# A linear-attention and soft-MoE kernel: a new start, a new task order, and the last expert's second layer split

## The chip, the core and the metric

The kernel runs on one core of a Trainium2 chip. The time is device microseconds of one execution; the figure for a kernel is the median of its runs. For the kernel before that is 119.74 us (three runs: 119.74, 120.53, 118.95).

## What is computed

An RWKV-like recurrence over 4 batches, 8 heads, 768 time steps and head size 48, and then a soft mixture of 8 experts with 4 slots each over the 3072 resulting rows of width 384:

```python
for t in range(S):
    cur = np.einsum('bhd,bhe->bhde', u[None] * kt, vt)
    y[:, :, t] = np.einsum('bhd,bhde->bhe', rt, state + cur)
    state = w[None, :, :, None] * state + np.einsum('bhd,bhe->bhde', kt, vt)
x = y as (3072, 384)
logits = x @ phi                                   # 3072 x 32
d = softmax(logits, over rows);  slot_input = d.T @ x
slot_out[e] = relu(slot_input[e] @ w1[e]) @ w2[e]  # w1 384 x 1024, w2 1024 x 384, 8 experts
c = softmax(logits, over slots)
out = c @ slot_out
```

All inputs are f32 in HBM, as is the output (3072 x 384, 4.7 MB). The inputs r, k, v are 14.2 MB and w1, w2 25.2 MB.

## The kernel before

The recurrence is done in chunks of 128 steps: twelve chunk steps `n` (`step`, L498), two batches at a time in the two halves of the partitions. Two chunks make a unit `U` (six units). Of each unit r, k and v are loaded by two loads each (36 loads of 128 x 768, `load`, L333), issued by POOL with a cast from f32 to bf16. `turned` (L438) transposes each 48-wide piece on TensorE (L447); VectorE multiplies the transposed k and r by tables of powers of w while it moves them out of PSUM (L458), ScalarE copies v (L455). Then, for each chunk: k and v are turned back per head (`normal`, L485), the scores k.r are made and masked (L512, L517), the current step's own term comes from u (L531, L563), y is summed in PSUM (L580 to L587) and copied to `x` (L594), the state is advanced (L543 to L557), `x` is transposed in three blocks of 128 columns (L609), copied (L612), and multiplied with phi into logits (L628). `tab`, the tables, hold the powers of w: w and u are loaded into `wu` (L344 to L347, twice each: for the two halves of the partitions), transposed by TensorE (L399), and their logarithm is multiplied by iota values and exponentiated (L407, L410). `ident_f`, the identity for transposes, is built by POOL (L352, L353).

`combine` makes the softmax over slots and its transpose `LexpT`; `dispatch` sums the slots' inputs over groups of chunks with a running maximum; `finish_slots` folds them into `uns` (L823, L828). `first_layer` (L863 to L889) makes `h` for two groups `g` of four experts and its transpose `hT`; its results stand in partitions 32j to 32j+31 for expert j of a group. `second_layer` (L905) multiplies `hT` by w2: for each of 8 y, four experts at a time, each in its own 32 columns of the array, all 384 wide, into one PSUM bank. ScalarE scales the sum by the slots' denominators into `so` (L910). `output` multiplies `LexpT` by `so` into 24 tiles of 128 x 384 (L934), which VectorE and ScalarE copy in turn (L936, L938) and SP stores in pieces of 1, 2, 3, 4, 4, 4, 4, 2 tiles (L940).

The weights are loaded by POOL as well, w1 first (L847) and then w2 (L850), 768 KB each in bf16, with a cast. w2 of expert e lies where loads 4e to 4e+3 of r, k, v lay. A load waits until the load 5 (or 7) places before it in the order of their creation has landed.

The order of all work is made by `Plan`: each piece is a `task` with a priority, an engine, a duration, what it reads, writes and uses. `order` runs a list schedule over these, with corrections per task in `TUNE`, and `emit` issues the tasks in the resulting order and puts fill matmuls (`idle`, L922) where TensorE would be free before the first chunk and after the last y.

Because every engine works through its own instructions in order, the order of emission is the order on each engine; POOL's loads stand in one row with its arithmetic (L471, L557).

Of the kernel before, what the change touches and what calls it, by code (L numbers as in the profile page):

```python
# [7 lines left out]
LAT = {"PE": 0.22, "DVE": 0.25, "ACT": 0.25, "POOL": 0.28, "SP": 0.1}  # L8
SAME = {"PE": 0.0, "DVE": 0.12, "ACT": 0.12, "POOL": 0.12, "SP": 0.0}


class Plan:
# [4 lines left out]
    def __init__(self, tune):  # L17

        self.tune = tune
        self.tasks, self.pools, self.writers, self.readers, self.users = [], {}, {}, {}, {}  # L20
        self.slot, self.landed = {}, []
# [30 lines left out]
    def order(self):  # L52
        tasks, free, end = self.tasks, {}, {}
# [8 lines left out]
        while ready:  # L62
            best = None
            for i in ready:
# [51 lines left out]
        return [i for _, _, i in sorted(out)]  # L116

    def emit(self, where, fill, took=0.22):
# [11 lines left out]
TUNE = {46: (0.6, 0.0), 47: (-0.81, 0.2), 48: (-0.47, 0.0), 49: (1.82, 0.0), 50: (-0.25, 0.2), 73: (-2.02, 0.0),   # L130
# [82 lines left out]
def kernel(  # L213
# [14 lines left out]
    C = 128  # L228
# [130 lines left out]
    for U in range(1, UU):  # L359
        for which in range(3):  # L360
            load(U, which)
# [28 lines left out]
    for b_ in banks:  # L390
        task(-150, "PE", 0.4, lambda b_=b_: clear(b_), r=["warm"], w=["cleared"], n=1)
# [600 lines left out]
```

## Time and profile before

| | us |
|---|---|
| median of 3 runs | 119.74 (118.95 to 120.53) |
| the profiled execution | 118.71 |
| its span | 116.9 |
| TensorE busy | 99.7 (85%) |
| VectorE busy | 92.9 (80%) |
| ScalarE busy | 78.4 (67%) |
| POOL busy | 72.6 (62%) |
| bytes moved by DMA (as written) | 24.70 MB |

The profiled execution's own time holds 1.8 us outside the span. Busy shares are means over stages: the recurrence up to about 84 us, a chain of small steps with the two layers up to about 101 us, and the output. A granted clock of 1.00 is TensorE's full speed. In the rows by stretch each engine's busy time comes with its instructions (x), then the granted clock, the share that the 16 DMA engines were busy (over 1 where transfers overlap), and GB/s written. A cast load reads twice the bytes that it writes.

### The profile page before, as it was taken

The page shows a single profiled execution, that of the slowest core. Times are in us where ns is not written, and L with a number is a line of the kernel's source. Part 1 is how long each engine was busy: PE and PEld are TensorE (multiplying, and loading weights), DVE is VectorE, ACT ScalarE, POOL GpSimd, SP SyncE. Part 2 cuts the span into 40 slices and gives each one's busy share as a digit, 9 for nine tenths or more (in the row PEclk, how much of TensorE's full clock was granted, in tenths as well). Part 3 has the DMA queues.
Part 4 walks back from the last instruction along what each step waited for, and adds up shares of the span by engine and source line. Part 5 has one row for each costly group of instructions (what it writes and reads, how often), then busy time and mean ns, then how long its engine had stood idle before and what let it go on. Part 6 is the DMA issues. An engine that isn't in the chain of part 4 may idle for free.

```text
span 116.9 us, 4280 instructions
## 1 busy us (share of the span) xinstructions
PE 99.7 (85%) x1844; PEld 71.7 (61%) x1844; DVE 92.9 (80%) x152; ACT 78.4 (67%) x159; POOL 72.6 (62%) x111
## 2 busy tenths in 40 slices
PE   5979999999998999999989998999899995655200
PEld 1354587778786788777868777787665552445100
DVE  6789599999999999999999899999975561086400
ACT  4261878788789697895888898889764750175400
POOL 6999848999999999894769945999111010000000
PEclk9999999999999999999999999999999999999955
DMA  2999999999999999999999999999999994059994
GB/s 10 171 187 198 208 206 205 209 205 209 206 207 209 230 209 212 223 210 221 214 208 224 210 220 210 214 219 216 208 219 216 210 219 98 0 196 410 419 421 170
DMA packets 9122, 24.70 MB, mean 211 GB/s; under 512 B 1424, under 2 KB 6160, under 8 KB 9104
## 3 DMA queue, kind: packets, MB, share of 16 engines
q0 software_dynamic: 7488, 19.66, 87.2%
q1 hardware_dynamic: 1584, 4.77, 10.4%
q8 instruction: 14, 0.23, 0.7%
q14 instruction: 4, 0.03, 0.1%
q10 hardware_dynamic: 32, 0.00, 0.0%
HBM read 39.38 MB, written 4.72 MB: 377 GB/s over the span
## 4 chain that ended last, share of the span: by engine, by line
PE 32%; POOL 27%; DMA 24%; issue 4%; DVE 4%; ACT 2%; DVEq 0%; POOLq 0%
DMA raw<-in_moe_w_dram 17%; POOL raw L339 12%; PE T L447 8%; POOL arena L471 7%; DMA raw<-in_k_dram 7%; POOL Z L557 5%; PE T L485 5%; PE Ab L512 3%; DVE arena L936 3%; PE Y L580 2%; PE T L609 2%; ACT arena L938 2%; PE Y L587 1%; PE Sb L531 1%; PE Y L585 1%
## 5 line engine op out<-in xcount | busy, mean ns | idle before, releaser
L458 DVE TENSOR_TENSOR arena<-T,tab 128x1024 bf16<-128x1024 bf16 x24 | 29.0, 1217 | 2.5 <-PE T L447 2.2
L517 DVE TENSOR_TENSOR arena<-Ab,mask 128x1024 bf16<-128x1024 f32 x24 | 29.2, 1216 | 0.9 <-PE Ab L512 0.8
L447 PE MATMUL T<-by_head,raw 128*48 128x128 bf16 x576 | 22.8, 221 | 1.2 <-DMA raw<-in_r_dram 0.7
L471 POOL TENSOR_TENSOR arena<-arena 128x1024 bf16<-128x1024 bf16 x10 | 21.4, 2136 | 0.6 <-DVE arena L458 0.5
L447 PEld LDWEIGHTS <-raw 128*48 128x48 bf16 x576 | 16.9, 102 | 6.4 <-issue 3.3
L557 POOL TENSOR_TENSOR Z<-Ss,wCm 128x384 bf16<-128x384 f32 x20 | 16.7, 841 | 5.1 <-ACT Ss L554 5.0
L455 ACT COPY arena<-T 128x1024 bf16<-128x1024 bf16 x12 | 12.2, 1017 | 3.7 <-PE T L447 3.5
L594 ACT CAST x_all<-Y 128x384 bf16<-128x384 f32 x23 | 11.1, 489 | 1.6 <-PE Y L587 1.5
L485 PE MATMUL T<-ident,arena 112*128 112x112 bf16 x176 | 12.0, 213 | 0.1
L554 ACT COPY Ss<-Y 128x384 f32<-128x384 f32 x20 | 9.7, 491 | 3.0 <-PE Y L547 2.7
L563 DVE TENSOR_TENSOR dv<-vn,Sb 128x768 bf16<-128x768 bf16 x12 | 11.3, 946 | 0.2
L489 ACT COPY vn<-T 128x768 bf16<-128x768 bf16 x12 | 9.7, 811 | 2.4 <-PE T L485 2.2
L612 ACT COPY xT<-T 128x768 bf16<-128x768 bf16 (+2 forms) x13 | 9.7, 758 | 1.3 <-PE T L609 1.0
L485 PEld LDWEIGHTS <-arena 112*128 112x128 bf16 x176 | 9.3, 97 | 1.5 <-DVE arena L458 0.3
L512 PE MATMUL Ab<-arena 48*128 48x128 bf16 x192 | 9.7, 219 | 0.3 <-issue 0.3
L664 POOL TENSOR_TENSOR Le<-E,rs 128x128 bf16<-128x128 f32 x6 | 2.4, 400 | 11.5 <-PE Ab L863 5.9
L580 PE MATMUL Y<-vn,arena 128*128 128x48 bf16 x192 | 8.8, 184 | 0.2 <-DVE arena L517 0.2
L489 ACT COPY kn<-T 128x768 bf16<-128x768 bf16 x10 | 8.0, 805 | 0.8 <-PE T L485 0.7
L339 POOL DMA_DIRECT2D raw<-in_k_dram x12 | 6.5, 554 | 2.4 <-DMA raw<-in_v_dram 1.4
L587 PE MATMUL Y<-dv,ident 128*128 128x384 bf16 x24 | 7.8, 325 | 0.0
L580 PEld LDWEIGHTS <-arena 128*128 128x128 bf16 x192 | 6.8, 96 | 1.4 <-DVE arena L517 0.3
L512 PEld LDWEIGHTS <-arena 48*128 48x128 bf16 x192 | 5.5, 94 | 3.1 <-issue 1.6
(146 smaller groups left out, 197.9 us busy)
## 6 DMA issues: line engine op xcount, KB each, us to landing
w_all<-in_moe_w_dram POOLq DMA_DIRECT2D x8, 768.0 KB, 17.7
raw<-in_moe_w_dram POOLq DMA_DIRECT2D x8, 768.0 KB, 20.6
out_dram<-arena SPq DMA_DIRECT2D x4, 768.0 KB, 5.6
raw<-in_k_dram POOLq DMA_DIRECT2D x12, 192.0 KB, 6.9
raw<-in_r_dram POOLq DMA_DIRECT2D x12, 192.0 KB, 7.0
raw<-in_v_dram POOLq DMA_DIRECT2D x12, 192.0 KB, 7.2
out_dram<-arena SPq DMA_DIRECT2D x2, 384.0 KB, 2.4
out_dram<-arena SPq DMA_DIRECT2D x1, 576.0 KB, 2.9
```

The costliest lines, as they stand in the source:

```text
L339: pool.dma_start(out=raw_of(which, U, x), in_=ap)), w=[("raw", 6 * U + 2 * which + x)], dma=0.97, lag=7)
L447: O(pe.transpose(T[64 * x:64 * x + D, C * j:C * j + C], raw_of(which, U, x)[:, jj * D:(jj + 1) * D], by_head[:]))
L455: O(act.copy(dst, src))
L458: O(dve.tensor_mul(dst.rearrange("p j (h c) q -> p j h c q", c=2), src.rearrange("p j (h c) q -> p j h c q", c=2), tb[:, :, :, None, :].to ...
L471: O((pool if U else dve).tensor_mul(pr_t[P["pr", 2 * U + b]].rearrange("p (h a) -> p h a", h=H), kt, rt))
L485: O(pe.transpose(T[:, h * C:h * C + 64 + D], cell(st[P[src, U]], h, cc)[0:64 + D], ident[0:64 + D, 0:64 + D]))
L489: O(act.copy(nt[P[name, n]][:].rearrange("p h x d -> p (h x) d")[:, :, 0:D], T[:].rearrange("p (a d) -> p a d", d=64)[:, :, 0:D]))
L512: O(pe.matmul(Ab[:, x, i * C:(i + 1) * C], cell(kt, 4 * rd + i, cc)[s], cell(rt, 4 * rd + i, cc)[s], start=True, stop=True))
L517: O(dve.tensor_mul(AT[:, :, 4 * rd:4 * rd + 4, :], Ab[:].rearrange("p x (h t) -> p x h t", h=4), mask[:, None, None, :].to_broadcast([128, ...
L557: task(n + 0.2 + 0.05 * hh, "POOL", 0.8, lambda hh=hh: O(pool.tensor_mul(Z_t[P["Z", (n, hh)]][:], Ss_t[P["Ss", (n, hh)]][:], wCm[:, 4 * hh ...
L563: O(eng.tensor_mul(dv_t[P["dv", n]][:].rearrange("p h x d -> p (h x) d"), vn_t[P["vn", n]][:].rearrange("p h x d -> p (h x) d"), sums[:, : ...
L580: O(pe.matmul(Y[:, (2 * i + x) * D:(2 * i + x + 1) * D], AT[:, x, h, :], vn[:, h, x, :], start=(i == 0 and x == 0), stop=False, skip_group ...
```

## The change

- **First v.** Load 4 of the 36 (v of the first unit, first batch) is issued by SP, without a cast, into f32 space in `AT_t[0]`, and cast by ScalarE into its place. It is SP's first instruction; phi follows. The other 35 are still POOL's.
- **w and u.** Each has its own tile, `w_in` and `u_in`, of 8 partitions, and comes by one load on ScalarE's queue that reads it twice; SP loads neither. They are transposed and copied each by itself, and the logarithm needs w alone.
- **ident_f** is built by POOL ahead of its first load, not behind the first two.
- **phi** is loaded with three consecutive rows per partition (128 pieces of 384 bytes in place of 384 of 128). So the transposes of x take every third column.
- **Order.** `TUNE` is empty; a list `SEQ` gives the order of all 613 tasks. On each engine it differs from before throughout. Among other things POOL's loads of r of the last unit stand ahead of r of the second unit; VectorE makes all four table products before its first product with data, and casts phi, clears x's ones, one `Le` and one `E` later, between the chunks; and only two clears of PSUM and a fill stand before w's transpose. The bank of `Sb` is cleared on a key of its own.
- **Last chunk's xT.** Its first third is copied by VectorE, and both parts of its transpose wait for both halves of x.
- **w2 of the last expert** is loaded in two parts, y 0 to 5 and y 6 to 7.
- **Second layer.** The fourth expert of each group is taken out of the row of four: its matmuls are made in two halves of 192 columns, into two other PSUM banks (`rest`), the other three as before (`most`). Behind the last part of w2 come two matmuls for each half. `so` is scaled in three pieces: 96 partitions by ScalarE, and the last 32 partitions half by ScalarE, half by VectorE.
- **Output.** The first tile is made and copied in two halves, by ScalarE and VectorE; the stores are of 1, 1, 1, 2, 3, 4, 4, 4, 4 tiles.

```diff
+            if i == 4:
+                st = AT_t[0].bitcast(f32)[:, 0:JD]
+                task(-220, "SP", 4.5, lambda ap=ap: O(sp.dma_start(out=st, in_=ap)), r=["sp"], w=["st", "sp"])
+                task(-95, "ACT", 0.83, lambda: O(act.copy(raw_of(2, 0, 0), st)), r=["st"], w=[("raw", 4)])
...
-    task(-200, "SP", 1.2, lambda: O(sp.dma_start(out=wu[0:8, 0, 0:D], in_=w)), r=["wu0"], w=["wuA"])
-    task(-200, "SP", 1.2, lambda: O(sp.dma_start(out=wu[8:16, 0, 0:D], in_=u)), r=["wu0"], w=["wuB"])
-    task(-200, "ACT", 1.2, lambda: O(act.dma_start(out=wu[0:8, 1, 0:D], in_=w)), r=["wu0"], w=["wuC"])
-    task(-200, "ACT", 1.2, lambda: O(act.dma_start(out=wu[8:16, 1, 0:D], in_=u)), r=["wu0"], w=["wuD"])
+    task(-210, "Q", 2.05, lambda: O(act.dma_start(out=w_in[:, :, 0:D], in_=both(w))), w=["wA"])
+    task(-210, "Q", 2.0, lambda: O(act.dma_start(out=u_in[:, :, 0:D], in_=both(u))), w=["uA"])
...
-                        O(pe.transpose(T[:, o:o + C], xx[:, x, mi * C:(mi + 1) * C], ident[:]))
+                        O(pe.transpose(T[:, o:o + C], xx[:, x, mi:Dm:nM], ident[:]))
...
+        def most(g, y0, y1):
+            for y in range(y0, y1):
+                for j in range(EL):
+                    O(pe.matmul(SO[32 * j:32 * j + 32, :], hT[g][:, y, 32 * j:32 * j + 32], w2_of(g * EG + j)[:, y, :],
+                                start=(g == 0 and y == 0), stop=(g == 1 and y == nF - 1), skip_group_check=True))
+        def rest(g, y0, y1, x):
+            s = slice(x * DH, (x + 1) * DH)
+            for y in range(y0, y1):
+                O(pe.matmul(Y_b[P[lk[x]]][RL:128, 0:DH], hT[g][:, y, RL:128], w2_of(g * EG + EL)[:, y, s],
+                            start=(g == 0 and y == 0), stop=(g == 1 and y == nF - 1), skip_group_check=True))
...
-        for sz in (1, 2, 3, 4, 4, 4, 4, 2):
+        for sz in (1, 1, 1, 2, 3, 4, 4, 4, 4):
```

More of the change, by code (lines that the diff above doesn't have):

```diff
@@ L6, with __init__ @@
 from concourse._compat import with_exitstack
-LAT = {"PE": 0.22, "DVE": 0.25, "ACT": 0.25, "POOL": 0.28, "SP": 0.1}
-SAME = {"PE": 0.0, "DVE": 0.12, "ACT": 0.12, "POOL": 0.12, "SP": 0.0}
+LAT = {"PE": 0.22, "DVE": 0.25, "ACT": 0.25, "POOL": 0.28, "SP": 0.1, "Q": 0.1}
+SAME = {"PE": 0.0, "DVE": 0.12, "ACT": 0.12, "POOL": 0.12, "SP": 0.0, "Q": 0.0}
+START = {"PE": 1.2, "DVE": 0.75, "ACT": 2.02, "POOL": 0.65, "SP": 0.0, "Q": 0.0}
 class Plan:
-    def __init__(self, tune):
-        self.tune = tune
+    def __init__(self, tune, seq=()):
+        self.tune, self.seq = tune, seq
         self.tasks, self.pools, self.writers, self.readers, self.users = [], {}, {}, {}, {}
@@ L63, in order @@
             best = None
-            for i in ready:
+            if self.seq:
+                i = self.seq[len(out)]
+                assert not wait[i]
+                eng, use = tasks[i][1], tasks[i][5]
+                at = max(since[i], free.get(eng, 0.0))
+                need = [k[0] for k in use if k not in self.slot]
+                for k in need:
+                    got = sorted(f for f in self.pools[k] if f is not None)
+                    at = max(at, got[need.count(k) - 1])
+                best = (at, 0.0, i, at)
+            for i in () if self.seq else ready:
                 prio, eng, _, _, _, use, _, _ = tasks[i]
@@ L115, in order @@
         self.spans = {i: (a, end[i]) for a, _, i in out}
-        return [i for _, _, i in sorted(out)]
+        return list(self.seq) or [i for _, _, i in sorted(out)]
     def emit(self, where, fill, took=0.22):
@@ L307, in w2_of @@
         return raw[e][:].rearrange("p a (b d) -> p (a b) d", d=Dm)
-    wu = sb("wu", [16, 2, 64], f32)
+    w_in, u_in = (sb(f"in_{t}", [H, 2, 64], f32) for t in "wu")
     phi_f = sb("phi_f", [128, nM, ES], f32)
@@ L336, in load @@
         for x in range(2):
+            i = 6 * U + 2 * which + x
             ap = src[2 * p + x, :, n * U2:(n + 1) * U2, :].rearrange("h (p j) d -> p h (j d)", j=J)
-            task(-101 if (U, which) == (0, 0) else -100 + U, "POOL", 0.54, lambda x=x, ap=ap: O(
-                pool.dma_start(out=raw_of(which, U, x), in_=ap)), w=[("raw", 6 * U + 2 * which + x)], dma=0.97, lag=7)
-    O(act.preload_act_table_set("natural_log_exp_and_others"))
-    task(-200, "DVE", 0.1, lambda: O(dve.memset(wu[:], 1.0)), w=["wu0"])
@@ new lines @@
+    O(act.preload_act_table_set("natural_log_exp_and_others"))
+    both = lambda m: m[:, None, :].to_broadcast([H, 2, D])
+    task(-210, "Q", 2.05, lambda: O(act.dma_start(out=w_in[:, :, 0:D], in_=both(w))), w=["wA"])
+    task(-210, "Q", 2.0, lambda: O(act.dma_start(out=u_in[:, :, 0:D], in_=both(u))), w=["uA"])
+    for t in (w_in, u_in):
+        task(-200, "DVE", 0.1, lambda t=t: O(dve.memset(t[:, :, D:64], 1.0)), w=["wu0"])
+    task(-200, "DVE", 0.3, lambda: O(dve.memset(warm[:], 0.0)), w=["warm"])
@@ L350 @@
+    task(-110, "POOL", 0.3, lambda: O(pool.memset(ident_f[:], 0.0)), w=["ident_f"])
+    task(-110, "POOL", 0.3, lambda: O(pool.affine_select(
+        out=ident_f[:], in_=ident_f[:], compare_op=ALU.not_equal, fill=1.0, base=0, pattern=[[-1, 128]],
+        channel_multiplier=1)), w=["ident_f"])
     load(0, 0)
     load(0, 1)
-    task(-100.5, "POOL", 0.3, lambda: O(pool.memset(ident_f[:], 0.0)), w=["ident_f"])
-    task(-100.5, "POOL", 0.5, lambda: O(pool.affine_select(
-        out=ident_f[:], in_=ident_f[:], compare_op=ALU.not_equal, fill=1.0, base=0, pattern=[[-1, 128]],
-        channel_multiplier=1)), w=["ident_f"])
@@ L356 @@
-    task(-100.5, "POOL", 0.5, lambda: O(pool.iota(R_i, pattern=[[1, J], [J, Q]], base=0, channel_multiplier=0)),
+    task(-99.5, "POOL", 0.5, lambda: O(pool.iota(R_i, pattern=[[1, J], [J, Q]], base=0, channel_multiplier=0)),
          w=["R_i"])
     load(0, 2)
+    task(-180, "SP", 0.6, lambda: O(sp.dma_start(out=phi_f[:], in_=moe_phi.rearrange("(p mo) s -> p mo s", p=128))),
+         r=["sp"], w=["phi_f", "sp"])
     for U in range(1, UU):
@@ L395, in warm_up @@
             task(prio, "PE", 0.25, lambda: clear(Y_b[1][:]), n=1, **kw)
-    warm_up(6, -94, r=["cleared"])
+    warm_up(2, -94, r=["cleared1"])
     warmed = len(P.tasks)
-    task(-95, "PE", 0.2, lambda: O(pe.transpose(Sb[:, 0:16], wu[:].rearrange("q a s -> q (a s)"), ident_f[0:16, 0:16])),
-         r=["wuA", "wuB", "wuC", "wuD", "ident_f", "cleared"], w=["wuTp"], use=[("S", "wu")], n=2)
-    task(-95, "DVE", 0.15, lambda: O(dve.tensor_copy(wuT[:], Sb[:, 0:16])), r=["wuTp"], w=["wuT"], use=[("S", "wu")])
-    task(-95, "ACT", 0.3, lambda: O(act.activation(out=lnw[:], in_=wuT[:, 0:H], func=AF.Ln)), r=["wuT"], w=["lnw"])
+    for i, t in enumerate((w_in, u_in)):
+        key, q = ("S", "wu"[i]), -95 + 20 * i
+        task(q, "PE", 0.2, lambda i=i, t=t: O(pe.transpose(Sb[:, 8 * i:8 * i + H], t[:].rearrange("q a s -> q (a s)"), ident_f[0:H, 0:H])),
+             r=["wu0", ("wA", "uA")[i], "ident_f", "cleared0"], w=[("wuTp", i)], use=[key], n=2)
+        task(q, "DVE", 0.15, lambda i=i: O(dve.tensor_copy(wuT[:, H * i:H * (i + 1)], Sb[:, 8 * i:8 * i + H])), r=[("wuTp", i)],
+             w=[("wuT", i)], use=[key])
+    task(-95, "ACT", 0.3, lambda: O(act.activation(out=lnw[:], in_=wuT[:, 0:H], func=AF.Ln)), r=[("wuT", 0)], w=["lnw"])
     def table(i, b):
@@ L841, with load_w @@
     so = sb("so", [128, Dm], bf)
-    FH, PH, YH = F // 2, C // 2, nF // 2
-    def load_w(e, second):
+    FH, PH, YH, YL = F // 2, C // 2, nF // 2, nF - 2
+    w2_first = {}
+    def load_w(e, second, part=0):
         lag = 7 if not second and e < 3 else 5
@@ L849, in load_w @@
         else:
-            task(-40 + e, "POOL", 0.57, lambda: O(pool.dma_start(
-                out=w2_of(e), in_=moe_w2[e].rearrange("(p y) d -> p y d", p=128))),
-                w=[("w2", e)] + [("raw", 4 * e + i) for i in range(4)], dma=3.7, lag=lag)
+            y0, y1 = (0, nF) if e < E - 1 else (YL if part else 0, nF if part else YL)
+            more = dict(w=[("w2", e, 1)], behind=w2_first[e]) if part else dict(
+                w=[("w2", e, 0)] + [("raw", 4 * e + i) for i in range(4)])
+            w2_first.setdefault(e, task(-40 + e + 10 * part, "POOL", 0.57, lambda: O(pool.dma_start(
+                out=w2_of(e)[:, y0:y1], in_=moe_w2[e].rearrange("(p y) d -> p y d", p=128)[:, y0:y1])),
+                dma=3.7 * (y1 - y0) / nF, lag=lag, **more))
     def first_layer():
@@ L898, in second_layer @@
         key = [("S", "so")]
+        lk = [("Y", "so0"), ("Y", "so1")]
         begins = None
-        for g in range(2):
-            for a in range(2):
-                def mm(g=g, a=a):
-                    for y in range(a * YH, (a + 1) * YH):
-                        for j in range(EG):
-                            O(pe.matmul(SO[32 * j:32 * j + 32, :], hT[g][:, y, 32 * j:32 * j + 32], w2_of(g * EG + j)[:, y, :],
-                                        start=(g == 0 and y == 0), stop=(g == 1 and y == nF - 1), skip_group_check=True))
-                i = task(60 + 2 * g + a, "PE", 0.7, mm, r=[("hT", g, a)] + [("w2", g * EG + j) for j in range(EG)], w=["SO"],
-                         use=key, n=16)
-                begins = i if begins is None else begins
@@ new lines, in rest @@
+        def rest(g, y0, y1, x):
[3 more added lines that the diff above has]
+                            start=(g == 0 and y == 0), stop=(g == 1 and y == nF - 1), skip_group_check=True))
+        for q, (g, y0, y1) in enumerate(((0, 0, YH), (0, YH, nF), (1, 0, YH), (1, YH, nF))):
+            i = task(60 + q, "PE", 0.04 + 0.165 * (y1 - y0), lambda g=g, y0=y0, y1=y1: most(g, y0, y1),
+                     r=[("hT", g, int(y0 >= YH))] + [("w2", g * EG + j, 0) for j in range(EL)], w=["SO"], use=key, n=EL * (y1 - y0))
+            begins = i if begins is None else begins
@@ new lines, in second_layer @@
+        for q, (g, y0, y1) in enumerate(((0, 0, nF), (1, 0, YL), (1, YL, nF))):
+            for x in range(2):
+                task(61.5 + q + 2 * (q > 0) + 0.1 * x, "PE", 0.03 + 0.083 * (y1 - y0), lambda g=g, y0=y0, y1=y1, x=x: rest(g, y0, y1, x),
+                     r=[("hT", g, a) for a in range(2)] + [("w2", g * EG + EL, int(q == 2))], w=[("SOl", x)], use=[lk[x]], n=y1 - y0)
+        task(80, "ACT", 0.55, lambda: O(act.mul(so[0:RL, :], SO[0:RL, :], rcs[0:RL, 0:1])), r=["SO", "rcs"], w=["so"], use=key)
@@ L911, in second_layer @@
+        task(81, "ACT", 0.35, lambda: O(act.mul(so[RL:128, 0:DH], Y_b[P[lk[0]]][RL:128, 0:DH], rcs[RL:128, 0:1])),
+             r=[("SOl", 0), "rcs"], w=[("so", 0)], use=[lk[0]])
+        task(81, "DVE", 0.35, lambda: O(dve.tensor_scalar(
+            out=so[RL:128, DH:Dm], in0=Y_b[P[lk[1]]][RL:128, 0:DH], scalar1=rcs[RL:128, 0:1], scalar2=None, op0=ALU.mult)),
+            r=[("SOl", 1), "rcs"], w=[("so", 1)], use=[lk[1]])
         return begins
@@ L929, in output @@
         i = 0
-        for sz in (1, 2, 3, 4, 4, 4, 4, 2):
+        for sz in (1, 1, 1, 2, 3, 4, 4, 4, 4):
             i0 = i
-            for _ in range(sz):
-                op = ob[i % 7][:, 0:Dm]
+            if i == 0:
+                for x, cp in enumerate((act.copy, dve.tensor_copy)):
+                    s = slice(x * Dm // 2, (x + 1) * Dm // 2)
+                    O(pe.matmul(ob[x][:, s], LexpT[:, 0:Nn:nN], so[:, s], start=True, stop=True))
+                    O(cp(obuf[:, 0, s], ob[x][:, s]))
+                i = 1
+            for _ in range(sz if i0 else 0):
+                op = ob[(i + 1) % 7][:, 0:Dm]
                 O(pe.matmul(op, LexpT[:, i:Nn:nN], so[:], start=True, stop=True))
```

33 lines of the change are left out of this document (18 added, 15 removed), and 104 rows, old and new, of tables (SEQ, TUNE).

## The prediction

> **What bounds it now.** I read the page first, then stretches of time, then the chain of waits backwards from the end. The page's slices give the busy share of the DMA engines; in the stretches the last three columns are the granted TensorE clock, the DMA share and GB/s written.
>
> ```profile
> span 116.9 us, 4280 instructions
> DMA  2999999999999999999999999999999994059994
> ```
>
> ```profile
> 2.00:2.50 0.50, 0.50 (x2) 0.15 (x1) 0.39 (x5) 0.02 (x1) 0.50 (x2) 1.00 0.04 5
> 2.50:3.00 0.50, 0.50 (x2) 0.15 (x1) 0.47 (x4) 0.00 (x0) 0.50 (x4) 1.00 1.33 46
> ...
> 3.50:4.00 0.50, 0.50 (x3) 0.22 (x2) 0.47 (x5) 0.17 (x2) 0.50 (x2) 1.00 1.01 184
> ...
> 30.00:40.00 10.00, 9.68 (x232) 7.52 (x230) 9.97 (x11) 8.58 (x14) 10.00 (x15) 1.00 1.17 213
> ...
> 98.50:99.00 0.50, 0.00 (x0) 0.00 (x0) 0.00 (x0) 0.00 (x0) 0.00 (x0) 1.00 0.42 94
> ...
> 106.00:108.00 2.00, 1.26 (x9) 1.01 (x8) 1.49 (x3) 1.60 (x4) 0.00 (x0) 1.00 1.05 420
> ```
>
> From about 3.5 us to 99 us the DMA engines are full with the casting loads (36 of r, k, v, 16 of weights); from then on bytes set the pace. The chain's end shows what follows when they are through:
>
> ```profile
> 80.06 19.59 DMA raw<-in_moe_w_dram
> ...
> 99.69 1.48 PE Sb L905 x29
> ...
> 101.19 0.59 ACT so L910
> ...
> 101.82 0.50 PE T L934 x2
> ```
>
> ```profile
> 102.83 8.01 SPq L940 DMA_DIRECT2D out_dram<-arena  x8
> ```
>
> The last w2 is issued at 80.06 and lands 19.6 us later, all of that in the queue, so its issue time is not what matters. After 99.64 nothing overlaps: 29 matmuls, the scaling `so`, the first output tile and, at 102.83, the first store. The stores then run at 420 GB/s to the end, so whatever moves 102.83 moves the end.
>
> The second bound lies close behind. In the middle stretch the columns are PE, PEld, DVE, ACT, POOL:
>
> ```profile
> 7.87:83.05 75.18, 72.23 (x1556) 56.39 (x1556) 71.92 (x82) 60.49 (x114) 64.58 (x89) 1.00 1.09 212
> 83.05:91.26 8.21, 8.15 (x81) 4.80 (x81) 5.61 (x18) 4.90 (x18) 0.80 (x2) 1.00 1.04 215
> ```
>
> From its first product with a table (7.87) to its last mask product (83.05) VectorE idles 75.18 - 71.92 = 3.26 us only. From 83.05 a latency chain of 8.2 us leads to `uns`, and TensorE arrives at the last expert here:
>
> ```profile
> 95.61 0.84 PE L905 MATMUL Sb<-raw,tab 128*32 128x384 bf16 x16
> ...
> 97.79 0.34 PE L905 MATMUL Sb<-raw,tab 128*32 128x384 bf16 x3
> ```
>
> At 97.79 it issues the first three experts of the second group and waits for the fourth until 99.69. Compute is thus about 1.6 us ahead of the DMA, no more.
>
> **The change, part by part.** The start first; times are start and duration.
>
> ```profile
> 1.02 0.59 ACTq L346 DMA_DIRECT2D wu<-in_w_dram  x1
> 1.26 1.25 POOL L339 DMA_DIRECT2D raw<-in_k_dram  x2 [0.81 <-POOLq L976]
> 1.80 0.41 SPq L348 DMA_DIRECT2D phi_f<-in_moe_phi_dram  x1
> 2.48 0.24 POOL L352 MEMSET ident_f<- 128x128 f32 x1
> 2.98 0.32 POOL L353 TENSOR_SCALAR_AFFINE_SELECT ident_f<-ident_f 128x128 f32<-128x128 f32 x1
> 5.08 0.17 DVE L401 COPY wuT<-Sb 128x16 f32<-128x16 f32 x1 [0.69 <-PE Sb L399]
> 5.54 1.90 DVE L407 TENSOR_TENSOR tab<-lnw,LexpT 128x512 f32<-128x512 f32 x3
> 7.87 1.22 DVE L458 TENSOR_TENSOR arena<-T,tab 128x1024 bf16<-128x1024 bf16 x1 [0.43 <-PE T L447]
> 9.01 0.28 DVE L427 TENSOR_TENSOR mask<-Sb,LexpT 128x128 f32<-128x128 f32 x1
> ```
>
> ```profile
> phi_f<-in_moe_phi_dram SPq DMA_DIRECT2D x1, 48.0 KB, 3.5
> ```
>
> *First v by SP.* It is 128 x 768 f32 = 393 KB; at the 420 GB/s of the f32 stores it takes 0.94 us. It is issued where SP issued w at about 1 us, so it can run before the casting stream, in a window where the share was 0.04. It takes 197 KB off the stream: 0.92 us at 213 GB/s. Against that POOL now builds `ident_f` (0.24 + 0.32) before its first load, so the stream begins about 0.5 us later. Net: the last weight lands 0.4 us earlier, at 99.2. Bounds: -0.92 if POOL's first issue hides the two instructions; +0.5 if the f32 load falls beside the stream and costs its 0.94 there. I take -0.4, since the window is empty. The extra cast on ScalarE lies in that engine's early idle time.
>
> The Trainium skill says under "DMA: Bandwidth & Descriptors", section "Issuing engines are not separate DMA queues", that loads from several engines share the same 16 DMA engines, so only issue time is saved. By that rule alone the f32 copy, twice the bytes written, would gain nothing; the row for 2.00:2.50 says that those engines were empty then.
>
> *w and u.* They leave ScalarE's queue at 1.02 as before; SP's half of them goes. With phi's 3.5 us to landing as the upper bound w is there by 4.5; I take 4.0, and two clears and a fill stand ahead of its transpose instead of eight clears. Then 0.4 for turn and copy, 0.3 for the logarithm, and four table products of 0.65: they end near 7.3, and the copy of u makes it 7.5. Before, three of four were done at 7.44, so the first data product gains little (7.5 for 7.87). But k, k, r, r now follow each other at 1.13 us (7.87 to 9.01) and end near 12.0, while before:
>
> ```profile
> 13.31 1.23 DVE L458 TENSOR_TENSOR arena<-T,tab 128x1024 bf16<-128x1024 bf16 x1 [1.16 <-PE T L447]
> ```
>
> the second r product ended at 14.54, after a stall of 1.16. So 2.5 us are won there.
>
> *Order.* VectorE gives part back: work once done early is now in its full stretch.
>
> ```profile
> L431 DVE CAST phi<-phi_f 128x32 bf16<-128x32 f32 x3 | 0.4, 176 | 0.0
> L379 DVE MEMSET Le<- 128x256 uint32 x2 | 0.5, 272 | 0.0
> L380 DVE MEMSET E<- 128x132 f32 x2 | 0.3, 168 | 0.1
> L612 ACT COPY xT<-T 128x256 bf16<-128x256 bf16 x1 | 0.4, 372 | 0.2 <-PE T L609 0.2
> ```
>
> Mask 0.28, phi 0.35 (three casts as issued), one Le 0.27, one E 0.17, two smaller memsets at most 0.34: 1.4. Left: 1.1 us. The rest of the order is unknown; before, the stretch has 3.26 - 1.16 = 2.1 us of other idle time. I take the same, with none and twice that as bounds: VectorE's last mask product between 3.2 us earlier and 1.0 later. POOL's new load order puts r of the last unit ahead of r of the second, 2 x 0.92 us later; those land near 16, VectorE wants them near 19: nothing. The last unit's split copy xT moves its 0.37 to VectorE, beside ScalarE: -0.3. Its transposes now wait for both halves of x; before they ran together too. Wide phi rows are 128 packets instead of 384, ahead of the stream: nothing.
>
> *Last expert.* Prices:
>
> ```profile
> L905 PE MATMUL Sb<-raw,tab 128*32 128x384 bf16 x64 | 3.5, 328 | 1.6 <-DMA raw<-in_moe_w_dram 1.6
> L922 PE MATMUL Y<-warm 128*128 128x512 bf16 x3 | 1.1, 382 | 0.0
> L910 ACT ACTIVATE so<-Sb,rcs 128x384 bf16<-128x384 f32 x1 | 0.6, 582 | 4.9 <-PE Sb L905 4.9
> L780 ACT ACTIVATE Db<-T 128x64 bf16<-128x64 f32 x1 | 0.2, 224 | 0.6 <-PE T L777 0.6
> L936 DVE COPY arena<-T 128x384 f32<-128x384 f32 x6 | 3.1, 549 | 5.0 <-PE T L934 5.0
> L938 ACT COPY arena<-T 128x384 f32<-128x384 f32 x6 | 2.7, 490 | 0.6 <-PE T L934 0.6
> ```
>
> ```profile
> 39.32 0.16 PE Y L587
> ```
>
> The 29 matmuls took 1.48: 0.33 latency and 28 spacings of 0.041, a quarter of the 0.16 that a lone 384-column matmul takes (L587), because four experts stream side by side. Three experts alone still take 0.16 per y: 48 matmuls cost what 64 did, 2.56. The fourth comes on top, 32 half-width matmuls of 0.08 in one column group: +2.56, of it 0.32 after the landing. Before the landing TensorE thus has to do 1.28 (group two, formerly behind the landing) + 2.24 more. Without any gain in VectorE's stream it is ready at 97.79 + 3.52 - 1.5 (three fills of 0.38 and a fourth like them that this work replaces) = 99.8; with the 1.1 + 0.3 won above, 98.4. So the landing at 99.2 decides, by 0.8 us.
>
> The Trainium skill, "TensorEngine Tiling (Array Packing)", section "Key Properties", states that column tiles load and multiply in parallel; this speaks against taking one expert out, and the 0.041 agrees with it.
>
> Behind the landing: four matmuls, 3 x 0.08 + 0.25 = 0.49 instead of 1.48 (-0.99). `so` of 192 columns: 0.22 to 0.58 for 64 to 384, so 0.37 instead of 0.59 (-0.22), the other half on VectorE beside it (some 0.35). First tile in halves: matmul 0.25 and copies of about 0.32 (less than 0.49 and 0.55), 0.65 to the store instead of 1.01 (-0.36). The nine stores of 1, 1, 1, 2, 3, 4... tiles are fed in time: a tile takes 0.47 us at 420 GB/s, two engines make one in about 0.27. Nothing; bounds -0.2 and +0.5.
>
> **Sum.** -0.4 - 0.99 - 0.22 - 0.36 = -2.0. The profiled execution took 118.71, 1.8 of it outside the span: 116.7. It lies 1.0 below the median of the runs shown (119.74) and under the lowest (118.95); from that median it would be 117.7. I forecast the middle, 117.2.
>
> **Rivals.** (1) TensorE, not the landing, sets the end, because the fourth expert lost its neighbours and VectorE's stream gained nothing: ready at 99.8, so 0.55 of the 2.0 is lost: 117.7. For it: slack of 1.6 against 3.5 of work; against: the stall of 1.16 at 13.31 goes.
> (2) Slower: the new order starves VectorE in its full stretch. Each idle microsecond beyond about 2.9 (2.1, and the 0.8 by which compute leads) moves the end by one; the 2.0 is eaten at 4.9, and 7.3 gives 2% slower, some 121. Nothing in the first rows of the new order shows such a stall, and TensorE's idle time of 2.95 in that stretch says how full an order can be.
> (3) The lead of SP's load is kept whole (-0.92): 116.7.
> (4) It does not do what it says: the f32 load falls beside the stream, landing +0.5: 118.1.
>
> **How the numbers follow.** Chances: forecast 0.46 (116.2 to 118.2), (1) 0.22 (117.2 to 118.7), (2) 0.12 (119.2 to 123), (3) 0.12 (115.4 to 117), (4) 0.08 (117.6 to 119). Two per cent, about what a measurement of this kernel can tell from no change, is 2.4 us, or 117.35: just over half of the forecast, most of (3) and some of (1) lie below. Faster 0.45, same 0.46, slower 0.09. Range 115.4 to 119.3.
>
> **What would show it.** Right: the four matmuls start at about 99.2 behind a DMA wait; first store near 100.8; no idle stretch on VectorE above 0.5 us between 8 and 80; second r product ends near 12. Wrong: the last four start with no wait on a DMA (rival 1), VectorE idle over 4 us (2), full DMA share not before 4.3 us (4).

## The result, and the profile after

The changed kernel is slower: 125.03 us median (123.92 to 125.73, 4 runs) beside 120.13 for the kernel before (118.95 to 121.35, 4 runs of the same session). The ratio is 1.0434, 95% interval 1.0303 to 1.0564. The profiled execution took 124.76, 123.0 of it in the span; the one before 118.71 and 116.9. Medians, here and below, are over all executions of a kernel; the ratios leave out those executions that ran some per cent longer at a lower granted clock.

The page of the changed kernel shows a hole in the DMA row that was not there before, besides the one before the stores:

```profile
span 123.0 us, 4304 instructions
DMA  2999999999991599999999999999999999149993
```

The stretches of the first part (columns as before: PE, PEld, DVE, ACT, POOL, granted clock, DMA share, GB/s):

```profile
7.87:83.05 75.18, 67.36 (x1482) 53.22 (x1483) 70.35 (x77) 54.19 (x100) 59.22 (x80) 1.00 1.02 193
18.00:26.00 8.00, 5.92 (x133) 4.48 (x132) 6.04 (x7) 4.73 (x9) 7.60 (x15) 1.00 1.16 208
...
37.00:38.00 1.00, 1.00 (x21) 0.87 (x21) 1.00 (x2) 0.44 (x2) 0.00 (x0) 1.00 0.29 51
38.00:39.00 1.00, 1.00 (x29) 0.75 (x25) 1.00 (x3) 1.00 (x4) 0.41 (x1) 1.00 0.02 3
39.00:40.00 1.00, 1.00 (x31) 0.76 (x27) 1.00 (x2) 0.34 (x2) 1.00 (x2) 1.00 0.00 0
40.00:41.00 1.00, 0.85 (x25) 0.67 (x23) 1.00 (x2) 0.91 (x2) 1.00 (x3) 1.00 0.06 16
```

VectorE looks almost as busy as before (70.35 us of 75.18, where it was 71.92), and that misleads. The groups of instructions show why. The row for the casts of phi was `0.4, 176` before; now it is

```profile
L402 DVE CAST phi<-phi_f 128x32 bf16<-128x32 f32 x3 | 4.3, 1436 | 0.0
```

The same three instructions take 4.3 us instead of 0.5 (3 x 176 ns) and count as busy all that time. The stretch of VectorE and of GpSimd in which they lie (start, duration):

```profile
25.57 0.17 DVE L402 CAST phi<-phi_f 128x32 bf16<-128x32 f32 x1
26.59 0.95 DVE L534 TENSOR_TENSOR dv<-vn,Sb 128x768 bf16<-128x768 bf16 x1 [0.85 <-PE Sb L502]
27.46 1.31 DVE L402 CAST phi<-phi_f 128x32 bf16<-128x32 f32 x1
...
30.96 2.83 DVE L402 CAST phi<-phi_f 128x32 bf16<-128x32 f32 x1
33.71 1.21 DVE L488 TENSOR_TENSOR arena<-Ab,mask 128x1024 bf16<-128x1024 f32 x1
```

```profile
26.07 2.14 POOL L442 TENSOR_TENSOR arena<-arena 128x1024 bf16<-128x1024 bf16 x1
28.15 0.56 POOL L306 DMA_DIRECT2D raw<-in_r_dram  x1
...
31.04 0.57 POOL L306 DMA_DIRECT2D raw<-in_k_dram  x1
31.56 2.19 POOL L442 TENSOR_TENSOR arena<-arena 128x1024 bf16<-128x1024 bf16 x1
```

The long casts lie beside a product of GpSimd (26.07 to 28.21, 31.56 to 33.75); the last ends 0.04 after it. The products alone do not account for all of it: the 1.31 us cast ends 0.56 after its product, about when the issue of a load ends, and the 2.83 us cast begins 0.60 before its product, while loads are issued. An issue by itself did not hold the first cast, which took 0.17 at 25.57, within issues that ran from 24.99 to 26.07. So what held the other two for about 1.1 of their 4.1 us is open; the starts and ends of GpSimd's records are rough. Everything behind comes late. TensorE and GpSimd, in that order:

```profile
34.98 0.40 PE L483 MATMUL Ab<-arena 48*128 48x128 bf16 x8 [2.43 <-DVE arena L488]
```

```profile
38.59 1.62 POOL L528 TENSOR_TENSOR Z<-Ss,wCm 128x384 bf16<-128x384 f32 x2 [4.39 <-ACT Ss L525]
40.15 1.08 POOL L306 DMA_DIRECT2D raw<-in_v_dram  x2
```

GpSimd waits 4.39 us for `Ss` ahead of its products Z, and the loads queued behind them are issued only at 40.15: that is the hole. The end of the kernel, TensorE's rows:

```profile
96.88 1.48 PE L840 MATMUL Y<-w_all,uns 128*32 128x512 bf16 x24
...
103.01 2.45 PE L884 MATMUL Sb<-raw,tab 128*32 128x384 bf16 x42
105.41 1.65 PE L890 MATMUL Y<-raw,tab 128*32 128x192 bf16 x16
107.39 0.42 PE L932 MATMUL T<-so,LexpT 128*128 128x192 bf16 x2 [0.34 <-ACT so L902]
```

The first expert layer begins at 96.88 (91.26 before, +5.6), the second layer ends at 107.06 with no wait for a landing, and the first store is issued at 108.37 instead of 102.83.

### The profile page after: what moved, and what is told of

It reads as the page before. It is cut to its first block, busy times and chain, and to the rows that moved or that the text cites. A ratio compares the mean times of both kernels' runs of the same rounds, so it can differ in the third digit from the quotient of the medians.

```text
span 123.0 us, 4304 instructions
## 1 busy us (share of the span) xinstructions
PE 101.2 (82%) x1854; PEld 73.5 (60%) x1854; DVE 96.4 (78%) x156; ACT 79.3 (64%) x161; POOL 73.0 (59%) x111
## 4 chain that ended last, share of the span: by engine, by line
PE 49%; DVE 15%; DMA 13%; issue 7%; POOL 6%; ACT 2%; DVEq 0%; POOLq 0%
PE T L418 9%; DMA raw<-in_r_dram 7%; DMA raw<-in_v_dram 6%; DVE arena L488 4%; PE Ab L483 4%; PE T L456 4%; POOL raw L306 4%; DVE dv L534 3%; PE Y L551 3%; DVE arena L939 3%; PE Ab L918 3%; PE T L580 2%; PE Y L890 2%; PE Sb L884 2%; PE Y L518 2%
## 5 line engine op out<-in xcount | busy, mean ns | idle before, releaser
L528 POOL TENSOR_TENSOR Z<-Ss,wCm 128x384 bf16<-128x384 f32 x20 | 16.7, 839 | 8.5 <-ACT Ss L525 8.4
L583 ACT COPY xT<-T 128x768 bf16<-128x768 bf16 (+1 forms) x12 | 9.4, 787 | 1.3 <-PE T L580 1.2
L556 PE MATMUL Y<-Z,arena 128*128 128x96 bf16 x80 | 6.8, 204 | 0.8 <-issue 0.8
```

The lines of the kernel that those rows point to most:

```text
L528: task(n + 0.2 + 0.05 * hh, "POOL", 0.8, lambda hh=hh: O(pool.tensor_mul(Z_t[P["Z", (n, hh)]][:], Ss_t[P["Ss", (n, hh)]][:], wCm[:, 4 * hh ...
```

## The experiments

Each kernel was timed beside the kernel before on the same chip; ratios are to that kernel.

**The casts.** Three kernels and one measurement by itself. First, the casts behind the copy of u:

```
+    ids = list(P.writers["phi_s"])
+    s = [i for i in P.seq if i not in ids]
+    at = s.index(P.writers[("wuT", 1)][0]) + 1
+    P.seq = s[:at] + ids + s[at:]
```

> The changed kernel with one thing moved back: the three casts of phi stand behind the copy of u into wuT, before the first data product, while GpSimd runs no tensor product. Theory (a cast from SBUF to SBUF on VectorE waits out a GpSimd product that runs): the three casts take about 0.17 us each; VectorE does not lose the 3.8 us at 27 to 34, Z L528 no longer waits 4.4 us for Ss, the hole in the DMA share at 37 to 41 shrinks or goes, and the time falls by 3 to 4.5 us, to 120.5 to 122. Rival (the new order starves VectorE by late loads and waits in any case, and the casts only fill idle time): within 1 us of the changed kernel, 124 to 126, and another wait takes the place of the casts.

120.54, ratio 1.0069 (1.001 to 1.0128): 3.6% of the time is gone with three instructions of 0.18 us, some 4.4 us. The wait at Z L528 is 0.93 instead of 4.39:

```profile
34.32 1.62 POOL L528 TENSOR_TENSOR Z<-Ss,wCm 128x384 bf16<-128x384 f32 x2 [0.93 <-ACT Ss L525]
```

Second, the casts where the change put them, but on ScalarE (`act.copy` for `dve.tensor_copy`):

> The changed kernel with the three casts of phi at the same place in the order, but on ScalarE. Theory (VectorE and GpSimd exclude each other, ScalarE and GpSimd do not): each cast takes 0.2 to 0.3 us although a GpSimd product runs beside it, the time falls by 2.5 to 4.5 us to 120.5 to 122.5. Rival 1 (the casts are slow because of the operands, or of a transfer, not because of VectorE's neighbour): they take over 1 us on ScalarE too, and the time stays at 124 to 126. Rival 2 (late loads rule): casts short, time unchanged.

120.75, ratio 1.0091 (1.0036 to 1.0146). The casts take 221 to 232 ns. One lies in the midst of a product (first row ScalarE, second GpSimd):

```profile
26.18 0.22 ACT L402 CAST phi<-phi_f 128x32 bf16<-128x32 f32 x1
```

```profile
24.73 2.19 POOL L442 TENSOR_TENSOR arena<-arena 128x1024 bf16<-128x1024 bf16 x1
```

So neither the operands nor the place are slow, but VectorE beside GpSimd. Third, the other way round, four extra casts in the kernel before:

```
+    for k_ in (("rT", 1, 1), ("rm", 0), ("rT", 3, 0), "cm"):
+        ... O(dve.tensor_copy(spare, phi_f[:, 0, :]))
```

> The kernel before with four extra casts of phi's first third into a spare tile, on VectorE, each at a place where a GpSimd product is under way (about 27.9, 34.7, 44.2 and 47.8); nothing else is changed and nobody waits for them. Theory: each takes until the product beside it ends, about 0.7 + 1.8 + 1.6 + 1.8, some 5 us of VectorE instead of 0.7; compute is ahead of the loads by 1.6 us only, so the time rises by 2.5 to 5 us, to 121.8 to 124. Rival (a cast is 0.17 us wherever it stands): 119.0 to 119.8.

123.92, ratio 1.0294 (1.0206 to 1.0382), some 3.5 us for four instructions. From the profiled execution (126.47) only the casts are read: 0.40, 2.04, 0.73 and 1.87 us. The first met no product but a Z of 0.85, and waited for that.

Last, which kinds of instruction wait:

> A measurement by itself; the reference's computation is left out (the output is zeros). VectorE runs one small instruction of a kind while a GpSimd product of 128x1024 bf16 (about 2.1 us, started by a one-element memset some 0.7 us earlier) is under way, and the same instruction with GpSimd idle, each three times; one row more has three casting loads being issued by GpSimd instead of a product. Theory (copies and casts from SBUF to SBUF wait until a running GpSimd product is over, other kinds go through): cast f32 to bf16 128x32, copy bf16 128x256 and copy f32 128x128 take 0.2 us alone and 1 to 1.8 us beside the product; memset, the copy from PSUM and the f32 product of two SBUF tiles take the same alone and beside it; the bf16 product of two SBUF tiles is open. Beside the issue of loads the cast takes 0.2. Rival (the stretch in the changed kernel came from something else): no kind differs by more than 0.2 us between alone and beside.

The rows of groups (mean ns before the second bar). Beside the product are L97, L91, L95, L86, L99 and L93; the same alone are L98, L92, L96, L88, L100 and L94:

```profile
L97 DVE TENSOR_TENSOR f<-f,f 128x128 f32<-128x128 f32 x3 | 5.4, 1787 | 0.0
...
L91 DVE COPY f<-f 128x128 f32<-128x128 f32 x3 | 5.2, 1722 | 0.0
L95 DVE TENSOR_TENSOR b<-b,b 128x256 bf16<-128x256 bf16 x3 | 5.0, 1670 | 0.1
L86 DVE CAST b<-f 128x32 bf16<-128x32 f32 x3 | 5.0, 1664 | 0.0
...
L99 DVE CAST b<-ps 128x256 bf16<-128x256 f32 x3 | 1.2, 414 | 0.0
L100 DVE CAST b<-ps 128x256 bf16<-128x256 f32 x3 | 1.2, 412 | 0.0
L96 DVE TENSOR_TENSOR b<-b,b 128x256 bf16<-128x256 bf16 x3 | 0.9, 291 | 0.1
L98 DVE TENSOR_TENSOR f<-f,f 128x128 f32<-128x128 f32 x3 | 0.8, 276 | 0.0
...
L92 DVE COPY f<-f 128x128 f32<-128x128 f32 x3 | 0.6, 216 | 0.0
...
L88 DVE CAST b<-f 128x32 bf16<-128x32 f32 x3 | 0.5, 171 | 0.0
L93 DVE MEMSET b<- 128x128 uint32 x3 | 0.5, 165 | 0.0
L94 DVE MEMSET b<- 128x128 uint32 x3 | 0.5, 165 | 0.0
```

Casts, copies and products whose operands all lie in SBUF wait the product out (1.4 to 1.5 us more each); memset and a cast that reads PSUM do not notice it. A cast that began together with the issue of a casting load took 171 ns. One expectation failed: the f32 product of two SBUF tiles waits too. A reduction of an SBUF tile, which this measurement does not have, took 0.27 us beside a product in the kernel with four extra casts (34.87, the product from 34.45 to 36.61). This fits that the kernel's heavy VectorE work, which reads T, Ab and Sb from PSUM, runs beside GpSimd's products: the row at 26.59 above takes 0.95 beside one, the same instruction at 34.84 takes 0.94 without.

**The hole in the DMA stream.** The last v pair and the first w1 ahead of the waiting Z, casts left in place:

```
+    ahead = [raw 34, raw 35, w1 0]   # moved in front of the two Z of step 2
```

> The changed kernel with the casts left where they are, but the last pair of v loads and the first w1 load moved ahead of the Z products in GpSimd's order, so that they do not stand behind its wait of 4.4 us for Ss. Theory (the time is lost on VectorE; at the end TensorE and not the last landing decides): the hole in the DMA share at 37 to 41 closes, the last weights land some 4 us earlier, and the time hardly moves, 124 to 125.5. Rival (the hole in the DMA stream of some 4 us is what costs the time): 120.5 to 121.5, with the casts still at 1.3 and 2.8 us.

124.78, ratio 1.0448 (1.0351 to 1.0546): no gain, but no test. The built program put these loads some 15 places ahead of where they were meant, TensorE waited 3.18 us at 20 to 23.5 for what they displaced, and a new hole came at 42. The three casts took 1.7 us there instead of 4.3, so they were not left as they were either. So the same with one-element copies on GpSimd that hold the loads in their place:

> The changed kernel, casts of phi as they are, with the last pair of v loads and the first w1 load ahead of the two Z products that wait, now held in that place by one-element copies on GpSimd (the first try put these loads some 15 places too early and starved the next ones). Theory (the time is lost on VectorE; the last second-layer matmuls of the changed kernel show no wait for a landing): the hole in the DMA share at 37 to 41 shrinks from 5 to 1.5 us or less, the last w2 lands earlier, and the time hardly moves, 124 to 125.5. Rival (the hole in the DMA stream costs the time): 120.5 to 122, with two casts still over 1 us.

124.15 (120.35 to 125.58, too scattered for an interval). In the profiled execution (125.58) the hole moved to 42 to 50 and kept its size, the casts took 4.5 us, and TensorE's granted clock was 0.50 from 36 to 40. One of the four took 120.35, as the rival said; no profile of it was kept, so whether its casts were short is not known. Neither theory is decided by these two; the next is cleaner, since the casts are out of the way.

> Casts early and the three loads ahead of the waiting Z products, both on the changed kernel. With the casts early alone (120.54) 2.3 us of stream were lost between 35 and 44, the last w2 landed near 101.2 and 16 matmuls waited 0.7 for it. Theory (the order's loads are what is left of the loss): the stream's loss falls below 1 us, the last landing comes before 100.2, the 16 matmuls start without a wait, time 119.4 to 120. Rival (what is left lies on VectorE and TensorE): time 120.3 to 121, no wait for the last landing either.

120.25, ratio 1.0045 (0.9989 to 1.0101). From 34 to 46 the stream writes 206 GB/s, where the row of casts early says 175, that of the changed kernel 114 and that of the kernel before 216. The loss of stream in these 12 us falls from 5.8 us to 2.3 and 0.6 (at 212 GB/s). The landing no longer decides, TensorE does (the 16 matmuls follow with no wait), and the medians differ by 0.3 us, within the intervals. So what was left of the hole once the casts were early cost little. What the whole hole cost beside the casts is not separated: moving the casts removed most of both.

**The start and the order of the loads.** The first v by GpSimd again, on casts early:

> The kernel with the casts early (120.54) with one more thing undone: the first v comes by GpSimd's casting queue again, ahead of its partner, and not by SP as f32 with a copy on ScalarE. The prediction's step (the f32 load takes 0.4 us net off the stream, bounds -0.92 to +0.5): the first k lands at about the same time, the stream is 0.4 us later at 34 us, the time 120.5 to 121.5. Rival (the f32 load falls beside the first casting loads and makes k land late, the first product at 8.76 instead of 7.87): k lands near 7.2, the first product starts before 8.2, the time 119.5 to 120.3.

120.35, ratio 1.0080 (1.0034 to 1.0127), the same. Yet the stream is behind. The stretch from 2 to 34, casts early and then this kernel:

```profile
2.00:34.00 32.00, 28.68 (x544) 20.21 (x546) 27.93 (x44) 21.51 (x35) 26.98 (x49) 1.00 1.13 206
```

```profile
2.00:34.00 32.00, 30.17 (x558) 20.76 (x558) 28.77 (x44) 20.97 (x36) 26.90 (x50) 1.00 1.11 192
```

Of the 206, 6 are the f32 copy's extra 197 KB; 8 GB/s over 32 us are 0.26 MB or 1.2 us of stream that SP's load wins in this pair of profiles. The row varies: the other kernels with SP's load write 199 to 208 there, so the gain may be almost nothing or up to 1.5 us. At 34 to 46 the order is reversed (175 with SP's load, 200 without), and the time is the same.

Then the two loads of the last unit's r, which the built program issues at 6.92, held back to their written place:

> Casts early (120.54), and the two loads of the last unit's r, which the built program issues as its fourth pair, held back to the place where the written order has them (by one-element copies on GpSimd). Theory (these 2 x 0.92 us of stream stand in front of r, v and k that VectorE wants at 17 to 26, against my prediction's 'nothing'): TensorE's waits for loads at 16 to 25 (0.43 r, 0.72 v, 0.69 v) go, VectorE's idle time between 18 and 26 falls from 2.35 us below 0.6, the time falls by 0.7 to 1.5 us, to 119.0 to 119.8. Rival (the stalls there have another cause, or the loads are missed later, behind the Z products): 120.2 or more.

119.42, ratio 1.0028 (0.9982 to 1.0075), and the waits are gone. The stretch from 18 to 26 in casts early, then with these loads held:

```profile
18.00:26.00 8.00, 6.38 (x149) 5.12 (x151) 5.65 (x6) 5.31 (x8) 7.59 (x13) 1.00 1.16 208
```

```profile
18.00:26.00 8.00, 8.00 (x188) 6.42 (x183) 7.93 (x10) 7.06 (x11) 7.70 (x10) 0.85 1.16 207
```

VectorE idles 0.07 us there instead of 2.35 (0 in the kernel before, 1.96 in the changed one). The granted clock was 0.85 in this execution (120.11, the kernel's median is 119.42), so TensorE's times in it are longer than in the others. The time follows by 0.4% only, within the intervals: in this profile the last landing decides, and the 16 matmuls wait 1.16 us for it.

**The tail.** The tail alone, on the kernel before:

> The kernel before with only the tail of the change: last w2 loaded in two parts, the last expert's slots in two banks of their own, the outputs in pieces of 1, 1, 1, 2, 3, 4. The prediction's theory (the last landing at 99.6 decides, four matmuls behind it instead of 29): last second-layer matmul ends near 100.2 and the first store is issued near 101.3, 1.3 to 1.6 us earlier than 102.83, time 118 to 118.9. Rival (the chain from uns to the last matmul, 10.2 us in the changed kernel against 9.9 before, decides as soon as the landing does not, since the fourth expert runs alone): last matmul at 101.2 to 101.5, only the quicker first tile is left, time 119.2 to 120.2.

118.37, ratio 0.9895 (0.9779 to 1.001): the time is inside the theory's range, but the profile shows the rival's way, in which nothing waits for a landing.

```profile
92.45 1.48 PE L869 MATMUL Y<-w_all,uns 128*32 128x512 bf16 x24
...
98.06 0.33 PE L913 MATMUL Sb<-raw,tab 128*32 128x384 bf16 x3
98.11 0.33 PE L919 MATMUL Y<-raw,tab 128*32 128x192 bf16 x2
98.23 0.33 PE L913 MATMUL Sb<-raw,tab 128*32 128x384 bf16 x3
...
100.12 0.99 PE L919 MATMUL Y<-raw,tab 128*32 128x192 bf16 x10
```

Here the order puts two of the lone expert's matmuls behind every three of the others, and they run beside them: 92.45 to 101.11 is 8.66 us, beside 9.91 - 1.55 of waiting = 8.36 in the kernel before. In the changed kernel 42 and then 16 run one behind the other, and the same way takes 10.18 us (9.88 with the casts early and the loads ahead).

With all four experts side by side and only the load split:

```
-  most(...) for three experts, rest(...) for the fourth, in a bank of its own
+  mm(g, y0, y1) for all four; only y = 6, 7 of group two wait for the second part
```

> The kernel before with the tail's loads and outputs (last w2 in two parts, scaling in halves by columns on two engines, outputs in pieces of 1, 1, 1, 2, 3, 4), but with the four experts of the second group side by side as before: only their last two y (8 matmuls) wait for the second part. Theory (taking one expert out of the packing costs TensorE what the split wins: 118.37 for the tail alone, where nothing waited for a landing): the last matmul ends 0.62 behind a landing near 99.9, at 100.5 instead of 101.1, the first store is issued near 101.9, time 117.6 to 118.1. Rival (both parts land together, or the chain before them decides): 118.2 to 118.8, as with the tail alone.

118.40, ratio 0.9911 (0.9868 to 0.9954). VectorE's half of the scaling began when ScalarE's had ended. So the scaling in one piece:

> The packed tail on the kernel before (118.40) with the scaling in one piece on ScalarE again. In that run VectorE's half of the scaling began only when ScalarE's half had ended (100.56 + 0.42, then 101.01 + 0.42), so the first tile's second half came 0.45 late. Theory (two halves out of one PSUM bank run one behind the other, so halving gains nothing): scaling 100.55 to 101.13, first store near 101.9 instead of 102.28, time 117.9 to 118.3. Rival: the first store stays at 102.2 or later, 118.4 or more.

117.98, ratio 0.9904 (0.9862 to 0.9945), not to be told from the last two by the ratio. Its profile shows the landing as the bound and the split at work:

```profile
98.82 1.46 PE L911 MATMUL Sb<-raw,tab 128*32 128x384 bf16 x29 [0.81 <-DMA raw<-in_moe_w_dram]
```

```profile
101.86 7.72 SPq L956 DMA_DIRECT2D out_dram<-arena  x9
```

The 29 start at the first part's landing, the second part comes while they run, and the first store is issued at 101.86 instead of 102.83. This version is about 1% faster than the kernel before.

At last the repairs together. Casts, loads and four experts side by side on the changed kernel:

> Casts early, the three loads ahead of the waiting Z products, and the last group's four experts side by side again (scaling in one piece), all on the changed kernel. The two repairs alone gave 120.25, with no wait for the last landing and 42 + 16 second-layer matmuls one behind the other from 97.97 to 101.72. Theory (what was left of the loss after the two repairs is the lone fourth expert at the end): last matmul at 100 to 100.6, time 118.4 to 119.3. Rival (what is left lies earlier in the new order): 119.7 or more.

119.50, ratio 1.0013 (0.9973 to 1.0052): as fast as the kernel before, between what the theory and the rival said. The way through the two layers:

```profile
92.69 1.48 PE L840 MATMUL Y<-w_all,uns 128*32 128x512 bf16 x24
...
100.11 1.48 PE L884 MATMUL Sb<-raw,tab 128*32 128x384 bf16 x32
```

It takes 8.90 us, 1.0 less than 9.88 with the fourth expert by itself in the same order, and 0.5 more than 8.36 in the kernel before. With the r loads held as well:

> The three repairs together (casts early, three loads ahead of the Z products, experts side by side: 119.50), and the two r loads of the last unit held back as well. Theory (with that the new order has no loss left that a load explains): VectorE idle between 18 and 26 below 0.6 us instead of 1.68, the fold's end and the last expert 1 to 1.5 us earlier, so that the last landing decides again, 117.8 to 118.6, as fast as the kernel before with the packed tail (117.98). Rival: 119.2 or more, the order itself costs it.

121.23, ratio 1.0151 (1.0074 to 1.0228), where 117.8 to 118.6 was expected. VectorE idles 0.81 us between 18 and 26 (1.69 without the holding; below 0.6 was expected). Five loads with their holding copies now stand ahead of the Z products in GpSimd's queue:

```profile
37.08 0.48 PE L514 MATMUL Y<-Z,ident 128*128 128x384 bf16 x1 [2.67 <-POOL Z L528]
```

A Z behind loads starves TensorE as a load behind Z starves the DMA engines. The copies took 0.48 us each with their waits, so this does not tell what the order without them would give.

## Why the prediction was wrong

The forecast said 117.2 and faster; 125.03 and slower was measured. The direction is that of the second rival (VectorE starved in its full stretch, 0.12, some 121); the mechanism of most of the loss is one that the prediction did not have.

- *"phi 0.35 (three casts as issued)"* is the step that failed. The durations came from a place where GpSimd ran no product (5.3 to 5.5) and were carried to one where it did. They took 4.31 us, and undoing that one move gave back some 4.4 of the 4.9 us. The Trainium skill, "SBUF — State Buffer", section "SBUF: two separate sides", states that VectorE and GpSimd share a pair of ports, which a GpSimd instruction or a VectorE instruction in a two-port mode or with two inputs in SBUF (the latter only against a GpSimd instruction that reads SBUF) holds to its end, and that whichever starts second blocks. The runs here agree (1664 ns beside a product, 171 alone), though no profile names the mode of the cast. That rule spoke against the change, and the prediction did not weigh it.
- *"VectorE idle over 4 us (2)"* does not show it. In the window from 7.87 to 83.05 VectorE idles 4.83 us, so the sign is there, but the casts' own 4.3 us are not in it, since an instruction that is held up counts as busy. By the prediction's own price (each microsecond beyond 2.9 moves the end) 4.83 would have eaten the forecast gain of 2.0 and no more. The mean duration of the group shows the rest.
- *"2.1 us of other idle time. I take the same"*, and of the last unit's r ahead of the second's: *"those land near 16, VectorE wants them near 19: nothing"*. Holding these loads back took 2.3 us of idle time off VectorE between 18 and 26, and 0.9 in the kernel with all repairs. The delay of 2 x 0.92 was charged to the second unit's r alone; the loads of v and k behind it come later as well. In the changed kernel TensorE waits 0.20 for an r at 17.46 and 0.72 for a v at 19.34.
- *First data product 7.5 for 7.87.* It came at 8.76, since k landed at 8.02. The four products then followed one another, as said, and ended at 13.45: 1.1 us won on 14.54, not 2.5. That is one execution: in casts early, with the same start but for the casts, k was there at 6.98 and the products ran from 7.71 to 12.43, 2.1 us won.
- *First v by SP, -0.4.* The one pair of profiles says 1.2 us of stream, beyond the bound of -0.92, but with a scatter as large as the term. Nothing of it was seen at the end (120.35 without it, 120.54 with it). Rival 4's sign did not show: the DMA share was full from 3.0 on.
- *"So the landing at 99.2 decides" and -0.99.* In the changed kernel TensorE decides. The whole way through the two layers is 0.3 longer where the order interleaves the lone expert with the others, and 1.8 in the changed kernel; of this some 1.0 to 1.3 goes when the four stand side by side in the same order (8.90 against 9.88 and 10.18), and 0.5 belongs to the rest of that order. The prediction's +2.56 took the matmuls as serial without looking whether the order lets them be. The first rival had this.
- *First tile -0.36.* In the tail alone 101.53 to 102.45, 0.92 instead of 1.01. The scaling's -0.22 was right (0.43 instead of 0.65, wait included).

The sum of what the profile shows: 3.8 for the casts and 2.0 for the r loads, less 1.1 at the start, are 4.7 of the 5.6 by which the first expert layer is late in these two executions. Open is how the last 1% divides, between the kernel with all repairs (1.0013) and the kernel before with the same tail (0.9904): the r loads are shown as a wait, not as a share of the time. Which of landing and TensorE decides also differs from execution to execution: two kernels that are the same up to there (the kernel before with the four experts side by side, scaling in two pieces and in one) begin the first expert layer at 92.44 and 91.13.

## What to carry to other kernels

A duration is only good for the neighbours it was measured beside: before a small VectorE instruction is moved, look at what GpSimd does at the new place and whether it is of a kind that was seen to wait (a cast, a copy or a product with all its operands in SBUF); if so, price it at the rest of GpSimd's instruction at least. Compare the mean durations of the same group in two profiles before comparing idle times, since a blocked instruction is booked as work. On a queue that both computes and issues loads, every wait is also a wait of the stream, and every load put ahead delays those behind it by its own transfer.

## What was not expected of the hardware

Two halves of one scaling, ScalarE's and VectorE's, out of one PSUM bank ran one behind the other (100.56 + 0.42, then 101.01 + 0.42, with the four experts side by side); out of two banks they overlapped (101.07 + 0.41 and 101.15 + 0.43, in the tail alone). In the first the trace names ScalarE's half as what VectorE's waited for, in the second the matmuls. So the trace shows a wait in the program; whether the bank would hold VectorE up without that wait was not tried.

In the kernel with loads too far ahead (its wait of 3.18 us) the granted TensorE clock (third column from the end) halved while TensorE waited, and stayed so for some 5 us after it had work again at 23.5:

```profile
21.00:22.00 1.00, 0.00 (x0) 0.00 (x0) 1.00 (x2) 0.43 (x1) 0.56 (x2) 1.00 1.13 198
22.00:23.00 1.00, 0.00 (x0) 0.00 (x0) 0.79 (x2) 0.00 (x0) 0.93 (x2) 0.51 1.15 204
23.00:24.00 1.00, 0.47 (x4) 0.29 (x4) 0.00 (x0) 0.00 (x0) 1.00 (x2) 0.50 1.17 209
...
27.00:28.00 1.00, 1.00 (x10) 0.54 (x6) 0.29 (x1) 1.00 (x2) 1.00 (x3) 0.50 1.03 210
```

Five us at half the clock are up to 2.5 us more of TensorE's time, an estimate from these rows.
